# Attention and two feed-forward layers on one core: the halves of each split put in successive half blocks

## The chip, the cores and the metric

The kernel runs on one core of a Trainium2 chip. The metric is the device time of one execution in microseconds (us), the median over repeated runs. The core's engines are TensorE (PE), VectorE (DVE), ScalarE (ACT), GpSimd (POOL) and SyncE (SP); POOL and SP issue this kernel's DMAs.

## The reference

Each of 8 batches and 8 heads pools 576 keys and values with 32 packed queries, and attends from 576 queries to the 32 pooled rows. The result, 4608 tokens of 512 features, runs through a gated layer (1536 wide) and a cosine layer (2048 wide). All is float32.

```python
p_packed = sm_attn(p, k, v)            # softmax(p k^T / 8) v
out = sm_attn(q, p_packed, p_packed)
x = out, laid out as (4608, 512)
g = x @ w_gate
x = (silu(g) * (x @ w_val)) @ w_out
h = x @ w_in
return (h * cos(h)) @ w_out2
```

## The kernel before

A float32 value is kept as two fast-format parts: `hi` is a rounded copy that ACT writes (L86), and `lo` is the value minus `hi`, which DVE writes (L87). `split` issues both, one behind the other. A product then takes three passes over the parts, except in batch 0, which multiplies plain float32. Weights arrive packed; ACT unpacks a tile in two instructions (`decode_a`, L93 and L94) and DVE finishes it in two (`decode_b`, L100 and L103).

The program has three stages. The first is a loop over the batches b = 0 to 7 (`a_up`). Each batch has 12 blocks f, and each block two half blocks: the products `pg` (gate) and `pv` (value), 12 matmuls each (L456; L445 in batch 0). ACT takes silu of `pg` (L469), DVE multiplies it with `pv` into `h` (L482), and POOL stores `h`. The weights of a batch are not the plain gate and value weights but these multiplied by the batch's pooled rows: a projection `wp` (L425) makes them for two blocks at once, and is split. In batch 0 the projection is made block by block (`a_wp0`, L410, copied at L417).

Between the half blocks, `side(k)` with k = 0 to 23 issues what a table of numbers gives for place k. That is the attention of batch b + 1, whose steps are: scores and their maximum (`s1_mm`, `s1_max`), the exponential (`s1_exp`, on ACT), transposes (`a_t`, L185), the pooling product (`a_pp`, L195, with its scaling `ppu` on DVE, L202), its transpose, the second scores with their softmax (`s2_*`) and a split. It is also the projections, the loads, and the preparation of the later weights, one `w2_step` at a time: a list of 130 items, each a decoding, a split with a store (`w2_put`), or sums of tiles on DVE (L365). 98 items run in the first stage: 15 in each of batches 1 to 6 and 8 in batch 7. The last 32 run in the second stage.

The second stage is a product by Strassen's scheme (L562): five sets of tokens (512 wide but the fourth, which is 256), seven products each. While one product runs, ACT and DVE split the operands `g` of the next. The third stage is the second layer; the change leaves it alone.

On each engine instructions run in the order in which the program issues them. Products of the first two stages write to four PSUM buffers of two banks each; a product may start when the reader of the buffer's former contents is done. A tile may be read or rewritten only when the instruction of the other engine that it depends on is done.

Of the kernel before, what the change touches and what calls it, by code (L numbers as in the profile page):

```python
# [10 lines left out]
F32 = mybir.dt.float32  # L11
F32R = mybir.dt.float32r
# [33 lines left out]
def attention_mlp_kernel(ctx: ExitStack, tc: tile.TileContext, qT, kT, vP, pP, wgv, w12, out):  # L46
# [38 lines left out]
    def split(src, hi, lo, eng=DVE):  # L85
        ACT.activation(out=hi, in_=src, func=AF.Copy)  # L86
        eng.tensor_tensor(out=lo, in0=src, in1=hi.bitcast(F32), op=ALU.subtract)  # L87

    def like(x, out):
# [99 lines left out]
    def a_pp(b):  # L189
        pp = bank2("pp")  # L190
        for r in range(2):
            et = ET.pop(r)
            for c in range(NC):
                for i in range(4):
                    PE.matmul(  # L195
                        out=pp[cols(i), r, :64],
                        lhsT=et[:, c, cols(i)],
                        rhs=vt[b, 2 * r + i // 2][:, c, rows(i % 2)],
                        start=(c == 0), stop=(c == NC - 1),
                    )  # L200
            ppu[r] = st.tile([128, 2, 64], F32, tag="ppu", name="ppu", bufs=2)
# [4 lines left out]
        for j in range(NPAIR):  # L206
            del vt[b, j]

# [115 lines left out]
    NITEM = NW1 + 2 * NF2  # L324
    w2_end = [NW1 + NF2]
    w2_bufs = {"r": (ups, 3), "s": (ups, 7), "p": (ups, 3)}
# [12 lines left out]

    def w2_put(w_, dst):  # L340
        n = w_.shape[1]
        p = w2_new([128, n, 2, 256], F32R, "p", "w2p")
        split(w_, p[:, :, 0, :], p[:, :, 1, :])
        nc.gpsimd.dma_start(out=dst.rearrange("n p c -> p n c"), in_=p.bitcast(F32).rearrange("p n x c -> p n (x c)"))  # L344

    def w2_put_d(w_, dst):
        p = w2_new([128, 2, 512], F32R, "p", "w2p")
        split(w_.rearrange("p n c -> p (n c)"), p[:, 0, :], p[:, 1, :])
        nc.gpsimd.dma_start(out=dst, in_=p.bitcast(F32))

    def w2_decode(i):
        def go():
            w2_load(i + 2)
            w_, t_ = w2_tile("w2f"), w2_tile("w2t")
            raw = w2_raw.pop(i)
            decode_a(raw, t_.rearrange("p n c -> p (n c)"), w_.rearrange("p n c -> p (n c)"))
            decode_b(raw, t_.rearrange("p n c -> p (n c)"), w_.rearrange("p n c -> p (n c)"))
            w2_f[i] = w_
        return go

    def w2_pair(into, i):
        sub_, add_ = ALU.subtract, ALU.add

        def tt(o_, x, y, op):
            DVE.tensor_tensor(out=o_, in0=x, in1=y, op=op)  # L365

        def left():
            w2_put(w2_f[i], into[0:2])
# [7 lines left out]
        def put_a():  # L376
            w2_put(w2_f["a"], into[3:5])

        def sums_b():
            a, s_ = w2_f[i], w2_f["a"]  # L380
            r = w2_f["b"] = w2_tile("w2c")
            tt(r[:, 0], s_[:, 1], a[:, 0], sub_)
            tt(r[:, 1], a[:, 1], r[:, 0], sub_)
            w2_put(w2_f[i + 1][:, 1:2], into[2:3])

        def put_b():
            w2_put(w2_f["b"], into[5:7])
            for key in (i, i + 1, "a", "b"):
                del w2_f[key]

        return [w2_decode(i), left, w2_decode(i + 1), sums_a, put_a, sums_b, put_b]
# [5 lines left out]
    for n in range(NF2):  # L397
        w2_todo += [w2_decode(NW1 + NF2 + n), lambda n=n: w2_put_d(w2_f.pop(NW1 + NF2 + n), w2d[n])]

    def w2_step():  # L400
        if w2_todo:
            w2_todo.pop(0)()

# [14 lines left out]

    def a_wp(b, m):
        if b >= B:  # L420
            return
        p_ = bank2("wp")
        for c in range(4):
            for r in range(2):
                PE.matmul(  # L425
                    out=p_[cols(c), r, :],
                    lhsT=pp_of(b, r, c),
                    rhs=wg[m, c // 2][rows(r), c % 2].rearrange("p a n -> p (a n)"),
                    start=True, stop=True,
                )  # L430
        w_ = wp[b, m] = ups.tile([128, 2, 2, 512], F32R, tag="w", name="wp", bufs=4)
        split(p_, w_[:, :, 0, :], w_[:, :, 1, :])

    def a_up(b, sched):
        def side(k):
            for s_ in sched.get(k, ()):
                s_()

        def half(f, o, name):
            p_ = bank2(name)  # L440
            if b == 0:
                w = wp[0, f]
                for c in range(2):
                    for u in range(2):
                        PE.matmul(  # L445
# [3 lines left out]
                        )  # L449
                return p_[:, :, :HS]  # L450
            w, o = wp[b, f // 2], o + 256 * (f % 2)
            for c in range(2):
                n = 0
                for u in range(2):
                    for x, y in PASSES:
# [5 lines left out]
                        n += 1  # L461
            return p_[:, :, :HS]

        for f in range(NF1):
            pg = half(f, 0, "pg")
# [3 lines left out]
            ACT.activation(out=s_, in_=pg, func=AF.Silu)  # L469
# [7 lines left out]
            side(2 * f)  # L477
            pv = half(f, 128, "pv")
# [3 lines left out]
            DVE.tensor_tensor(out=h_, in0=s_, in1=pv, op=ALU.mult)  # L482
            nc.gpsimd.dma_start(out=h1[f, :, S * b:S * b + S], in_=h_.rearrange("p c n -> p (c n)"))  # L483
# [168 lines left out]
    with tc.manual_schedule():  # L652
# [25 lines left out]
        u_step(1, 1)  # L678
        a_pp(0)
        a_ppt(0)  # L680
        u_step(2, 1)
# [34 lines left out]
        def attention(sched, b, at_k):  # L716
            steps = (
                (lambda: s1_mm(b), lambda: s1_max(0), lambda: s1_max(1)), (s1_exp,), (s1_sum,), (a_t,),
                (lambda: a_pp(b),), (lambda: a_ppt(b),),
                (lambda: s2_mm(b), lambda: s2_turn(0), lambda: s2_turn(1)),  # L720
                (s2_max,), (s2_sub,), (s2_exp,), (s2_sum,), (s2_mul,), (lambda: s2_back(b),),
                (lambda: s2_split(b),), (lambda: a_wp(b, 0),), (lambda: a_wp(b, 1),),
            )
# [4 lines left out]
        for b in range(B):  # L728
            sched = {}
            if b == 0:  # L730
                for k, what in ((0, "k"), (2, "v"), (6, "q")):
                    put(sched, k, loads(1, what))
                attention(sched, 1, (3, 3, 6, 6, 8, 10, 12, 13, 14, 14, 16, 17, 18, 19, 20, 22))
                for k, what in ((12, "k"), (16, "v"), (20, "q")):
                    put(sched, k, loads(2, what))
                put(sched, 23, lambda: w2_load(0), lambda: w2_load(1))
            else:
                for m, k in ((2, 2), (3, 5), (4, 9), (5, 14)):
                    put(sched, k, lambda m=m: a_wp(b, m))
                if b < B - 1:  # L740
                    attention(sched, b + 1, (0, 1, 4, 4, 7, 8, 11, 12, 13, 13, 15, 16, 17, 18, 18, 21))
                    for k, what in ((6, "k"), (12, "v"), (16, "q")):
                        put(sched, k, loads(b + 2, what))
                    for k in (1, 2, 3, 4, 5, 6, 7, 8, 9, 10, 19, 20, 21, 22, 23):
                        put(sched, k, w2_step)
                else:
                    stage["att"].close()
                    late["da"] = pool("da")
                    for k in range(8):
                        put(sched, k, w2_step)  # L750
                    put(sched, 0, lambda: load_w1(0), lambda: g_first.append(new_g(512)), lambda: load_h(0, 0, 0))
# [16 lines left out]
        w2_end[0] = NITEM  # L768
        w2_load(NW1 + NF2)
        w2_load(NW1 + NF2 + 1)  # L770
        x_now = [None] * 7
# [4 lines left out]
        for s_ in range(len(SETS)):  # L776
            end = s_ == len(SETS) - 1
            for i in range(7):
# [249 lines left out]
```

## Time and profile before

| what | value |
|---|---|
| time, median of 3 runs (lowest to highest) | 1524.75 us (1523.59 to 1526.01) |
| the profiled execution: its time, its span | 1522.2 us, 1520.4 us |
| PE busy over the span | 1465.4 us (96%) |
| DVE busy | 1087.6 us (72%) |
| ACT busy | 850.2 us (56%) |
| DMA queue of SP, share of 16 engines | 51.8% |

Shares are averages over three stages with different limits. Ends of matmuls are modelled, so starts are the better measure on PE. A wait is put down to the releaser that came last.

### The profile page before, as it was taken

How to read it: one execution, taken by the hardware profiler on the slowest of the kernel's cores; microseconds unless marked ns; L12 is line 12 of the kernel's file. 1: busy time of each engine (PE TensorE's matmuls, PEld its weight loads, DVE VectorE, ACT ScalarE, POOL GpSimd, SP SyncE). 2: the span in 40 equal slices, each digit the busy share in tenths (PEclk: the TensorE clock that was granted, in tenths of full speed). 3: DMA queues.
4: the chain of work that ended last, by engine and by line, in shares of the span. 5: the costliest groups of instructions: out<-in, count | busy, mean ns of one | idle time of the engine just before them, and what ended most of it. 6: DMA issues, size and time to landing. Idle time of an engine off the chain costs nothing.

```text
span 1520.4 us, 25197 instructions
## 1 busy us (share of the span) xinstructions
PE 1465.4 (96%) x9432; PEld 1262.3 (83%) x9432; DVE 1087.6 (72%) x1767; ACT 850.2 (56%) x1501; POOL 123.9 (8%) x230
## 2 busy tenths in 40 slices
PE   8999899899899999999999999999999999999998
PEld 6667777777789788887888999999989998998997
DVE  6767776776775888988886775776776586677654
ACT  5765654565654455555475555555555464565642
POOL 0011221212221011011000000000000000000000
PEclk9999999999999999999999999999999999999999
DMA  8946855846588576466296586576667558656641
GB/s 317 341 169 231 292 210 196 307 178 226 208 300 326 219 253 246 156 215 242 92 381 215 172 257 225 176 226 198 201 208 254 167 175 284 199 174 193 203 157 42
DMA packets 140937, 335.64 MB, mean 221 GB/s; under 512 B 15248, under 2 KB 25488, under 8 KB 140816
## 3 DMA queue, kind: packets, MB, share of 16 engines
q1 hardware_dynamic: 120720, 262.19, 51.8%
q0 software_dynamic: 20096, 71.84, 12.2%
q8 instruction: 75, 1.23, 0.3%
q14 instruction: 46, 0.38, 0.1%
HBM read 252.71 MB, written 81.26 MB: 220 GB/s over the span
## 4 chain that ended last, share of the span: by engine, by line
PE 65%; issue 7%; DVE 5%; DMA 3%; ACT 3%; POOL 1%; SPq 0%; POOLq 0%; DVEq 0%; ACTq 0%
PE acc L891 26%; PE p L876 22%; PE o L562 14%; PE pg L456 2%; PE pv L456 1%; DMA hr<-h 1%; POOL h L483 1%; DMA w<-w1u 1%; DVE h L482 1%; POOL w2u L344 1%; DMA w2u<-w2p 1%; DVE wp L87 0%; DVE w2f L100 0%; PE wp L425 0%; DVE p L575 0%
## 5 line engine op out<-in xcount | busy, mean ns | idle before, releaser
L891 PE MATMUL acc<-wd,g 128*128 128x512 f32 x1728 | 418.1, 391 | 0.0
L876 PE MATMUL p<-xs,up 128*128 128x384 f32 x2016 | 379.5, 339 | 2.4 <-ACT p L951 1.9
L891 PEld LDWEIGHTS acc<-wd,g 128*128 128x128 f32 x1728 | 323.0, 188 | 61.4
L876 PEld LDWEIGHTS p<-xs,up 128*128 128x128 f32 x2016 | 358.9, 188 | 14.7 <-ACT p L951 2.8
L562 PE MATMUL o<-g,w 128*128 128x512 f32 (+1 forms) x1260 | 266.5, 373 | 7.2 <-DVE g L87 3.9
L562 PEld LDWEIGHTS o<-g,w 128*128 128x128 f32 x1260 | 220.6, 189 | 52.9 <-DVE g L87 5.5
L854 ACT ACTIVATE t<-c,quarter 128x384 f32<-128x384 f32 x144 | 88.6, 615 | 198.3 <-DVE c L964 192.6
L456 PEld LDWEIGHTS pv<-a,wp 128*128 128x128 f32 x1008 | 138.7, 189 | 26.3 <-DVE h L482 7.6
L86 ACT ACTIVATE g<-hr 128x1024 fp32r<-128x1024 f32 (+1 forms) x105 | 102.0, 976 | 101.4 <-PE o L562 54.1
L456 PE MATMUL pv<-a,wp 128*128 128x288 f32 x1008 | 152.7, 301 | 5.5 <-DVE h L482 4.9
L456 PEld LDWEIGHTS pg<-a,wp 128*128 128x128 f32 x1008 | 138.8, 189 | 21.1 <-issue 8.3
L456 PE MATMUL pg<-a,wp 128*128 128x288 f32 x1008 | 152.5, 300 | 0.3 <-DVE h L482 0.3
L87 DVE TENSOR_TENSOR g<-hr,g 128x1024 fp32r<-128x1024 f32 (+1 forms) x105 | 113.6, 1112 | 32.7 <-ACT g L86 32.5
L959 DVE TENSOR_TENSOR u<-v,p 128x384 f32<-128x384 f32 x48 | 26.6, 553 | 120.1 <-PE p L876 119.7
L864 DVE TENSOR_TENSOR g<-t,g 128x384 fp32r<-128x384 f32 x192 | 105.7, 550 | 8.6 <-ACT g L851 8.5
L469 ACT ACTIVATE silu<-pg 128x576 f32<-128x576 f32 x96 | 62.3, 649 | 82.8 <-PE pg L456 70.5
L856 DVE TENSOR_TENSOR t<-t,k 128x384 f32<-128x384 f32 x192 | 105.8, 551 | 3.5 <-ACT k L860 1.8
L857 ACT ACTIVATE t<-t 128x384 f32<-128x384 f32 x192 | 98.1, 511 | 2.5 <-DVE t L856 2.4
L851 ACT ACTIVATE g<-t 128x384 fp32r<-128x384 f32 x192 | 98.7, 514 | 0.4 <-DVE t L862 0.4
L905 DVE TENSOR_TENSOR oacc<-oacc,acc 128x512 f32<-128x512 f32 x108 | 73.7, 683 | 34.6 <-PE acc L891 34.6
L860 ACT ACTIVATE k<-t 128x384 int32<-128x384 f32 x192 | 98.1, 511 | 0.0
L87 DVE TENSOR_TENSOR wp<-wp 128x1024 fp32r<-128x1024 f32 x42 | 51.3, 1221 | 51.8 <-ACT wp L86 51.7
(101 smaller groups left out, 1488.4 us busy)
## 6 DMA issues: line engine op xcount, KB each, us to landing
up<-w2u SPq DMA_DIRECT2D x336, 256.0 KB, 3.1
wd<-w2d SPq DMA_DIRECT2D x96, 512.0 KB, 6.3
h<-h POOLq DMA_DIRECT2D x96, 288.0 KB, 4.7
hr<-h SPq DMA_DIRECT2D x48, 512.0 KB, 7.2
raw<-in_w SPq DMA_DIRECT2D x44, 512.0 KB, 4.8
raw<-in_wgv SPq DMA_DIRECT2D x24, 512.0 KB, 7.9
w2u<-w2p POOLq DMA_DIRECT2D x24, 512.0 KB, 5.1
w<-w1u SPq DMA_DIRECT2D x21, 512.0 KB, 11.2
```

The costliest lines, as they stand in the source:

```text
L86: ACT.activation(out=hi, in_=src, func=AF.Copy)
L87: eng.tensor_tensor(out=lo, in0=src, in1=hi.bitcast(F32), op=ALU.subtract)
L456: PE.matmul(out=p_[:, c, :HS], lhsT=w[:, u, x, o:o + 128], rhs=a2[b][:, u, y, HS * c:HS * c + HS], start=(n == 0), stop=(n == 5),)
L562: PE.matmul(out=acc[:, m, :N], lhsT=wd1[n, fp][:, j, 256 * x + 128 * m:256 * x + 128 * m + 128], rhs=g1[n, fp][:, y, j, :], start=(first a ...
L851: ACT.activation(out=three["g"][:, 0, :], in_=three["t"], func=AF.Copy)
L854: ACT.activation(out=now["t"], in_=now["h"], func=AF.Identity, scale=1.0 / TWO_PI, bias=quarter)
L856: DVE.tensor_tensor(out=one_["t"], in0=one_["t"], in1=one_["k"], op=ALU.subtract)
L857: ACT.activation(out=one_["t"], in_=one_["t"], func=AF.Sin, scale=SIN_SCALE)
L860: ACT.activation(out=now["k"], in_=now["t"], func=AF.Copy)
L864: DVE.tensor_tensor(out=three["g"][:, 1, :], in0=three["t"], in1=three["g"][:, 0, :].bitcast(F32), op=ALU.subtract)
L876: PE.matmul(out=out, lhsT=w[:, u, 128 * k:128 * k + 128], rhs=x[:, v, k, :], start=(first and k == 0 and i == 0), stop=(last and k == 1 an ...
L891: PE.matmul(out=acc, lhsT=gs[p, a, t][:, x, o:o + 128], rhs=wd[j, f][:, y, :], start=(f == 0 and n == 0), stop=(f == 3 and n == 2),)
```

## The change

Each split and each decoding of the first stage, and the preparation of the later weights in both stages, is issued in two parts. ACT's instruction is issued at its place k; DVE's instruction and the store behind it are issued at the next place (`pend`) or at the next `w2_step` (`w2_flush`). The scaling of the pooling product becomes a step of its own, behind all 80 matmuls of that product. Attention has 20 steps in place of 16, at other places. In batch 0 projections are made for two blocks at once from block 2 on, and the first block's four products with the first half of the features come ahead of those with the second half. Of the list of 130 items, 110 now run in the first stage (17 in each of batches 1 to 6, 8 in batch 7); the 20 that are left run in the first three sets of the second stage, one to a product, and none in the last two sets.

```diff
+    def split_later(src, hi, lo, then=None):
+        ACT.activation(out=hi, in_=src, func=AF.Copy)
+
+        def go():
+            DVE.tensor_tensor(out=lo, in0=src, in1=hi.bitcast(F32), op=ALU.subtract)
+            if then:
+                then()
+        return go
...
     def a_pp(b):
-        pp = bank2("pp")
+        pp = s1_["pp"] = bank2("pp")
...
+    def a_ppu():
+        pp = s1_.pop("pp")
+        for r in range(2):
             ppu[r] = st.tile([128, 2, 64], F32, tag="ppu", name="ppu", bufs=2)
...
     def s2_split(b):
...
-            split(s2_["af"], a2[b][:, :, 0, :], a2[b][:, :, 1, :])
+            pend.append(split_later(s2_["af"], a2[b][:, :, 0, :], a2[b][:, :, 1, :]))
...
-    w2_end = [NW1 + NF2]
+    w2_end = [NW1 + NF2 + 6]
...
             decode_a(raw, t_, w_)
-            decode_b(raw, t_, w_)
-            w2_f[i] = w_
+            return lambda: decode_b(raw, t_, w_)
...
     def w2_step():
+        w2_flush()
         if w2_todo:
-            w2_todo.pop(0)()
+            w2_dve.append(w2_todo.pop(0)())
...
     def a_wp(b, m):
...
-        split(p_, w_[:, :, 0, :], w_[:, :, 1, :])
+        pend.append(split_later(p_, w_[:, :, 0, :], w_[:, :, 1, :]))
 
     def a_up(b, sched):
         def side(k):
+            now = pend[:]
+            del pend[:]
+            for s_ in now:
+                s_()
             for s_ in sched.get(k, ()):
                 s_()
...
-                if f + 1 < NF1:
-                    a_wp0(f + 1)
+                if f == 0:
+                    a_wp0(1)
+                elif f % 2:
+                    if f + 1 < NF1:
+                        a_wp0_pair((f + 1) // 2)
...
-                    attention(sched, b + 1, (0, 1, 4, 4, 7, 8, 11, 12, 13, 13, 15, 16, 17, 18, 18, 21))
+                    attention(sched, b + 1, (0, 1, 2, 5, 6, 8, 9, 10, 12, 13, 14, 15, 16, 18, 19, 20, 21, 17, 19, 22))
...
-                    for k in (1, 2, 3, 4, 5, 6, 7, 8, 9, 10, 19, 20, 21, 22, 23):
+                for k in (0, 3, 4, 5, 5, 6, 7, 7, 8, 9, 10, 11, 11, 12, 17, 21, 23) if b < B - 1 else range(8):
...
-                if s_ or i > 2:
-                    for _ in range(2 if i in (1, 6) else 1):
-                        w2_step()
+                if s_ < 3 or i < 3:
+                    w2_step()
```

The order of instructions shows the move at three places, all in batch 3. First DVE around the first projection of the batch; the names are those of the words above, `mx` and `nm` the maxima of the scores, `w2f` a decoded tile. Before, from `h` of block 0:

```order
L482 TENSOR_TENSOR h<-silu,pv 128x576
L100 SCALAR_TENSOR_TENSOR w2f<-w2t,w2f 128x512
L103 SCALAR_TENSOR_TENSOR w2f<-raw,w2f 128x512
L87 TENSOR_TENSOR wp<-wp 128x2x512
L365 TENSOR_TENSOR w2c<-w2f 128x256 x2
L482 TENSOR_TENSOR h<-silu,pv 128x576
L87 TENSOR_TENSOR w2p<-w2c,w2p 128x2x256
```

Now, from `h` of block 1:

```order
L550 TENSOR_TENSOR h<-silu,pv 128x576
L99 TENSOR_TENSOR w2p<-w2c,w2p 128x2x256
L115 SCALAR_TENSOR_TENSOR w2f<-w2t,w2f 128x512
L118 SCALAR_TENSOR_TENSOR w2f<-raw,w2f 128x512
L550 TENSOR_TENSOR h<-silu,pv 128x576
L99 TENSOR_TENSOR wp<-wp 128x2x512
L115 SCALAR_TENSOR_TENSOR w2f<-w2t,w2f 128x512
L118 SCALAR_TENSOR_TENSOR w2f<-raw,w2f 128x512
L99 TENSOR_TENSOR w2p<-w2f,w2p 128x2x256
```

The row `wp<-wp`, which needs ACT's copy of the same projection, stood behind a decoding that needs ACT too, and ahead of `h` of block 1. Now it stands behind `h` of block 2, one half block after the copy, and two decodings stand around it.

Second, ACT at the same place. Before, from silu of block 0 to that of block 2:

```order
L469 ACTIVATE silu<-pg 128x576
L169 ACT_TABLE_LOAD
L169 ACTIVATE E,sm<-s_2429,nm 128x576
L169 ACTIVATE E,sm<-s_2430,nm 128x576
L93 ACTIVATE w2t<-raw 128x512
L94 ACTIVATE w2f<-raw,low_87 128x512
L469 ACT_TABLE_LOAD
L469 ACTIVATE silu<-pg 128x576
L86 ACTIVATE wp<-wp 128x2x512
L86 ACTIVATE w2p<-w2c 128x2x256
L469 ACTIVATE silu<-pg 128x576
```

Now, from silu of block 1 to the copies in block 2:

```order
L530 ACTIVATE silu<-pg 128x576
L184 ACT_TABLE_LOAD
L184 ACTIVATE E,sm<-s_2406,nm 128x576
L184 ACTIVATE E,sm<-s_2407,nm 128x576
L108 ACTIVATE w2t<-raw 128x512
L109 ACTIVATE w2f<-raw,low_87 128x512
L530 ACT_TABLE_LOAD
L530 ACTIVATE silu<-pg 128x576
L108 ACTIVATE w2t<-raw 128x512
L109 ACTIVATE w2f<-raw,low_87 128x512
L96 ACTIVATE wp<-wp 128x2x512
L96 ACTIVATE w2p<-w2f 128x2x256
L96 ACTIVATE w2p<-w2f 128x256
```

The exponential with its two table loads comes one half block later, a second decoding stands ahead of the projection's copy, and two copies for stores follow it.

Third, PE at the pooling product, with what each row waits for (`DVE_49` and `Activation_49` are signals of DVE and ACT, `PE_49` of PE itself, `DMAHW` of loads). Before:

```order
L195 MATMUL pp<-vt,ET 32x64 [waits DMAHW3_49,DVE_49]
L195 MATMUL pp<-vt,ET 32x64
L195 MATMUL pp<-vt,ET 32x64 [waits DMAHW4_49]
L195 MATMUL pp<-vt,ET 32x64 x17
L195 MATMUL pp<-vt,ET 32x64 [waits DMAHW5_49,DVE_49]
L195 MATMUL pp<-vt,ET 32x64
L195 MATMUL pp<-vt,ET 32x64 [waits DMAHW6_49]
L195 MATMUL pp<-vt,ET 32x64 x17
L456 MATMUL pg<-a_2282,wp 128x288 [waits Activation_49]
```

Now:

```order
L210 MATMUL pp<-vt,ET 32x64 [waits DMAHW5_49,Activation_49]
L210 MATMUL pp<-vt,ET 32x64
L210 MATMUL pp<-vt,ET 32x64 [waits DMAHW6_49]
L210 MATMUL pp<-vt,ET 32x64 x17
L210 MATMUL pp<-vt,ET 32x64 [waits DMAHW7_49,Activation_49]
L210 MATMUL pp<-vt,ET 32x64
L210 MATMUL pp<-vt,ET 32x64 [waits DMAHW0_49]
L210 MATMUL pp<-vt,ET 32x64 x17
L510 MATMUL pv<-a_2336,wp 128x288 [waits PE_49]
```

The second half of the product waited for DVE, which had to read the first half out of the same buffer; now it waits for ACT's copy of the transposes.

## Rows read from the trace of the kernel before

**Rows 1.** Busy time by window: us, PE, PEld, DVE, ACT, POOL, granted clock, DMA
```profile
26.00:96.80 70.80, 64.79 (x557) 41.93 (x557) 53.13 (x82) 52.99 (x82) 6.33 (x13) 0.98 0.82 287
96.80:442.00 345.20, 313.93 (x3242) 261.95 (x3241) 246.72 (x378) 198.11 (x287) 73.96 (x133) 0.99 0.64 228
485.80:660.00 174.20, 172.79 (x747) 140.12 (x747) 148.84 (x154) 95.55 (x120) 17.90 (x33) 1.00 0.63 226
660.00:712.00 52.00, 46.19 (x311) 42.03 (x310) 43.90 (x66) 30.18 (x52) 8.68 (x16) 0.97 0.75 271
```

**Rows 2.** Waits of PE, 96.8 to 442 us: total, times, longest
```profile
PE pp L195 <- DVE ppu L202: 10.4, 6, 2.1
PE wp L425 <- ACT silu L469: 7.0, 5, 1.8
PE tp L185 <- DVE wp L87: 5.6, 6, 1.4
```

**Rows 3.** Waits of DVE for ACT, same stretch and columns
```profile
DVE wp L87 <- ACT wp L86: 48.2, 21, 4.1
DVE w2p L87 <- ACT w2p L86: 15.5, 17, 2.3
DVE w2f L100 <- ACT w2f L94: 15.0, 9, 3.0
DVE a L87 <- ACT a L86: 7.4, 6, 1.2
```

**Rows 4.** Timeline of PE, batch 3: start, us, instructions, idle before
```profile
222.59 0.77 PE L185 MATMUL tp<-ident,E 128*128 128x128 f32 x5 [1.41 <-DVE wp L87]
223.92 3.25 PE L456 MATMUL pv<-a,wp 128*128 128x288 f32 x12 [0.56 <-DVE h L482]
227.10 1.09 PE L425 MATMUL wp<-wg,ppT 64*32 64x512 f32 x16
251.92 1.76 PE L456 MATMUL pg<-a,wp 128*128 128x288 f32 x12
253.52 1.76 PE L456 MATMUL pv<-a,wp 128*128 128x288 f32 x12
```

**Rows 5.** Timeline of ACT, batch 4, and two rows of DVE
```profile
266.79 1.01 ACT L86 ACTIVATE wp<-wp 128x1024 fp32r<-128x1024 f32 x1
267.69 0.66 ACT L93 ACTIVATE w2t<-raw 128x512 f32<-128x512 f32 x1
268.91 0.64 ACT L469 ACTIVATE silu<-pg 128x576 f32<-128x576 f32 x1
275.04 1.28 ACT L169 ACT_TABLE_LOAD   x1 [1.91 <-DVE nm L161]
276.33 0.74 ACT L169 ACTIVATE E<-s,nm 128x576 f32<-128x576 f32 x1
277.90 1.28 ACT L469 ACT_TABLE_LOAD   x1
...
269.32 0.68 DVE L100 SCALAR_TENSOR_TENSOR w2f<-w2t,w2f 128x512 uint32<-128x512 uint32 x1
280.80 1.23 DVE L87 TENSOR_TENSOR wp<-wp 128x1024 fp32r<-128x1024 f32 x1 [3.61 <-ACT wp L86]
```

**Rows 6.** Waits of PE, 485.8 to 712 us, and one row of its timeline
```profile
PE o L562 <- DVE g L87: 3.9, 5, 1.4
PE o L562 <- ACT g L86: 3.3, 2, 2.2
...
706.64 0.49 PE L562 MATMUL o<-g,w 128*128 128x512 f32 x1 [2.16 <-ACT g L86]
```

**Rows 7.** Timeline of PE in batch 0
```profile
28.68 2.80 PE L445 MATMUL pg<-af,wpf 128*128 128x288 f32 x6 [1.93 <-DVE af L277]
62.14 0.66 PE L410 MATMUL wp<-wg,ppT 64*32 64x256 f32 x16
93.99 1.09 PE L425 MATMUL wp<-wg,ppT 64*32 64x512 f32 x16
```

More of the change, by code (lines that the diff above doesn't have):

```diff
@@ L200, in a_pp @@
                     )
+        for j in range(NPAIR):
+            del vt[b, j]
+    def a_ppu():
+        pp = s1_.pop("pp")
+        for r in range(2):
             ppu[r] = st.tile([128, 2, 64], F32, tag="ppu", name="ppu", bufs=2)
@@ L383, in sums_b, with right_and_sums @@
             tt(r[:, 1], a[:, 1], r[:, 0], sub_)
[L384 to L391, printed above, removed]
+            del w2_f[i], w2_f[i + 1]
+        right = w2_put(lambda: w2_f[i + 1][:, 1:2], into[2:3])
+        def right_and_sums():
+            lo = right()
+            return lambda: (lo(), sums_a())
+        return [
+            w2_decode(i), w2_decode(i + 1), w2_put(lambda: w2_f[i], into[0:2]), right_and_sums, lambda: sums_b,
+            w2_put(lambda: w2_f.pop("a"), into[3:5]), w2_put(lambda: w2_f.pop("b"), into[5:7]),
+        ]
     for n in range(NP1):
@@ L396, in attention_mlp_kernel, with w2_flush @@
         w2_todo += w2_pair(w2u[n], NW1 + 2 * n)
-    for n in range(NF2):
-        w2_todo += [w2_decode(NW1 + NF2 + n), lambda n=n: w2_put_d(w2_f.pop(NW1 + NF2 + n), w2d[n])]
+    for n in range(0, NF2, 2):
+        i = NW1 + NF2 + n
+        w2_todo += [w2_decode(i), w2_decode(i + 1), w2_put_d(i, w2d[n]), w2_put_d(i + 1, w2d[n + 1])]
+    w2_dve = []
+    def w2_flush():
+        while w2_dve:
+            w2_dve.pop(0)()
     def w2_step():
+        w2_flush()
         if w2_todo:
-            w2_todo.pop(0)()
+            w2_dve.append(w2_todo.pop(0)())
     wp = {}
@@ L417, in a_wp0, with a_wp0_pair, wp_mm @@
         ACT.activation(out=wp[0, f], in_=p_[:, :, :256], func=AF.Copy)
-    def a_wp(b, m):
-        if b >= B:
-            return
+    wp0 = []
+    def a_wp0_pair(m):
+        if not wp0:
+            wp0.append(ups.tile([128, 2, 2, 512], F32, tag="a2", name="wpp", bufs=2))
+        p_ = wp_mm(0, m)
+        w_ = wp0[0][:, m % 2]
+        ACT.activation(out=w_, in_=p_, func=AF.Copy)
+        for f in (2 * m, 2 * m + 1):
+            wp[0, f] = w_[:, :, 256 * (f % 2):256 * (f % 2) + 256]
+    def wp_mm(b, m):
         p_ = bank2("wp")
@@ L430, in a_wp, with half @@
                 )
+        return p_
+    def a_wp(b, m):
+        if b >= B:
+            return
+        p_ = wp_mm(b, m)
         w_ = wp[b, m] = ups.tile([128, 2, 2, 512], F32R, tag="w", name="wp", bufs=4)
-        split(p_, w_[:, :, 0, :], w_[:, :, 1, :])
+        pend.append(split_later(p_, w_[:, :, 0, :], w_[:, :, 1, :]))
     def a_up(b, sched):
         def side(k):
+            now = pend[:]
+            del pend[:]
+            for s_ in now:
+                s_()
             for s_ in sched.get(k, ()):
                 s_()
-        def half(f, o, name):
-            p_ = bank2(name)
+        def half(f, o, p_, us=(0, 1)):
             if b == 0:
                 w = wp[0, f]
-                for c in range(2):
-                    for u in range(2):
+                for u in us:
+                    for c in range(2):
                         PE.matmul(
@@ L461, in half @@
                         n += 1
-            return p_[:, :, :HS]
         for f in range(NF1):
-            pg = half(f, 0, "pg")
+            first = b == 0 and f == 0
+            pg = bank2("pg")
+            if first:
+                pv = bank2("pv")
+                half(f, 0, pg, (0,))
+                half(f, 128, pv, (0,))
+                half(f, 0, pg, (1,))
+            else:
+                half(f, 0, pg)
             if b == 0 and f:
@@ L477, in a_up @@
             side(2 * f)
-            pv = half(f, 128, "pv")
+            if first:
+                half(f, 128, pv, (1,))
+            else:
+                pv = bank2("pv")
+                half(f, 128, pv)
             if b == 0 and f:
```

81 lines of the change are left out of this document (45 added, 36 removed).

## The prediction

> **What bounds the kernel now.** I read the windows by stage first, then the waits of PE, then those of DVE in the stretch that the change rewrites, and last the timelines there.
>
> The windows [rows 1] show where PE stands still. Batches 1 to 6 take 345.2 us, in which PE is busy for 313.9: 31.3 idle, the largest lump in the run. Batch 0 has 6.0 (70.8 less 64.8), the first three sets of the second stage 1.4, and the window round its narrow fourth set 5.8. The third stage is not touched. The granted clock is 0.99 and 0.97 where PE waits most.
>
> The waits of PE [rows 2] name the 31.3: the pooling product's second half for DVE's `ppu` (10.4, six times), projections for ACT's silu (7.0), transposes for DVE's `lo` of a projection (5.6), and smaller ones of the same kind. So DVE and ACT free the PSUM buffers late. Why, when DVE is busy for only 246.7 of 345.2 us? Its waits for ACT [rows 3] answer: 48.2 + 15.5 + 15.0 + 7.4 = 86.1 us it stands in front of the `lo` half of a split or the second half of a decoding. 246.7 + 86.1 is 332.8 of 345.2. DVE has no slack in this stage: it works through its queue in order, and the hand-over from ACT inside the queue is its loss. That is the loss the change goes for.
>
> A second price hangs on the waits. After the gaps of 1.41 and 0.56 us in batch 3, a `pv` half block takes 3.18 us from start to start (223.92 to 227.10) where an undisturbed one takes 1.60 [rows 4]. That is the lower of the two clock levels, 1.2 in place of 2.4 GHz. 1.6 us is one such loss; the mean clock of 0.99 over 345.2 us allows up to 3.5. I take 3.0 for batches 1 to 6, and for the fourth set 0.03 x 52.0, 1.6 us, by its row in [rows 1].
>
> **Batches 1 to 6.** At stake: 31.3 + 3.0 = 34.3 us. Removed for certain is the wait inside the pooling product: all 80 matmuls are issued before DVE reads the buffer, so the 10.4 go [rows 2]. What is added is two list items per batch: a decoding (two of 0.68, 1.3 with their overlap) and a split of half the width of the 1.23 in [rows 5] are 2 us of DVE, far less than the 86.1 / 6 = 14.4 us per batch that it stood waiting. DVE's work still fits under PE's 52 us a batch (313.9 / 6).
>
> What is late next? I walked batch 3 through the three queues with durations of the timelines; two places stay. The first is the exponential. Let T = 0 be the end of block 1's `pg`. ACT then does silu (0.64), a table load (1.28), two exponentials (276.33 to 277.90, 1.57), a decoding (267.69 to 268.91, 1.22), the load back (1.28), silu of block 2, a second decoding (1.22), and only then the copy of the projection (1.01) [rows 5]: 0.64 + 1.28 + 1.57 + 1.22 + 1.28 + 0.64 + 1.22 + 1.01 = 8.9. DVE's `lo` adds 1.23 [rows 5] and frees the buffer at 10.1. PE meanwhile does `pv`, `pg`, the projection, `pv`, `pg` (four half blocks at 1.60, 1.09 for the projection) and ten transposes (1.4, by 0.77 for five less overlap) [rows 4]: 8.9. The next `pv` needs that buffer and waits 1.2; with the time that signals take on ACT's and DVE's side I count 1.4.
>
> The second is a hand-over the other way. Behind the projection's copy ACT has two copies for stores, and the second needs a tile that DVE decodes behind that same `lo`: DVE is ready at 10.1 + 1.3 = 11.4 [rows 5]. ACT, whose first copy is half as wide as the 1.01, has been free since 9.4. It stands for 2.0, then does the second copy (a quarter, 0.3) and silu of block 3, done at 12.4. `pg` of block 4, due at 10.1 + 1.6 = 11.7, waits 0.7. Elsewhere the walk finds 0.3, in all 2.4 us in this batch. Its position in the list is the heaviest one: two decodings in this spot; the other batches have one or none there. I take 2.0 a batch, 12.0 in all. No row shows the new order, so the bounds are 0 (all buffers in time) and 5.0 a batch, 30 in all (nearly today's 31.3 / 6 = 5.2). **Gain 34.3 - 12.0 = 22.3.**
>
> Here a page of the Trainium skill speaks against the change. The row first: after the load at 275.04, lasting 1.28, the exponential starts at 276.33 [rows 5], so a switch of tables costs 1.3 us. "ScalarE: Activation LUTs", section "What ACT_TABLE_LOAD costs", counts a drain of about 1.38 us on top of a load of 1.283 for every switch. By that estimate the first place, with two switches ahead of the copy, would wait 2.8 longer in each batch, and six batches would give back 16.6 of the gain. The trace does not show the drain, and the sum goes by the row.
>
> **Batches 0 and 7.** Eleven single projections of 0.66 become one single and five double ones of 1.09 [rows 7]: 7.3 less 6.1 is 1.2, or less with overlap; I take 0.9. One projection moves from batch 7 to batch 0, at no net cost. The first block's wait of 1.93 for the features [rows 7] gets three more products ahead of it, half a us each (eight matmul rows in some 2 us): 1.5 gained. Against it the double projection needs block 3's weights decoded two blocks early, which I reckon at 2.0 of new wait, between nothing and the four instructions of a decoding twice over, 5. Of the idle time of batch 0 that is not the 1.93 (4.1) I take 1.5 as gone, since the pooling product no longer waits inside and ACT copies less; batch 7 gives 0.3. **Gain** 0.9 + 1.5 - 2.0 + 1.5 + 0.3 = **2.2**, between -2 and 6.
>
> **The second stage.** PE waits 7.2 there for the operands `g`, 3.9 for DVE and 3.3 for ACT [rows 6]; 5.8 of it lies round the fourth set [rows 1], whose products are half as long while the list costs DVE the same. Nine of the 32 items ran there before, none does now. The load of the next set's tokens, issued when DVE frees their tile, moves ahead with them, and the wait at 706.64 (2.16) is for it [rows 6]. I take 5.0 of 5.8, and 1.0 of the 1.6 of clock. The first products now carry items that they didn't: one a product is hidden, since DVE is busy for 148.8 of 174.2 us there and the items fell from 23 to 20 in these three sets. If that cover is gone, a decoding's 1.3 us shows at up to three products. **Gain 6.0**, between 2 and 8.
>
> **The sum.** 22.3 + 2.2 + 6.0 = 30.5. The profiled execution took 1522.2 us (span 1520.4), so 1491.7; the median of the runs shown is 2.55 above it, so I forecast 1494.
>
> **The rivals.** *ACT becomes the late engine.* It has lost nothing of its four table loads per batch, and the places found above are both its own. If every batch loses 4.5 and not 2.0, 15 us of gain go: 1509. For it speaks the walk, against it that ACT is busy for only 198.1 of 345.2. The page above would do just this, by its own figures: 1511.
>
> *The waits only move.* DVE's halves are later than before by half a block, so buffers are held longer, and PE loses elsewhere what it got from the pooling product. The second stage's 6.0 stay: 1518. Against it: 86 us of standing cannot stay if ACT's halves are ahead.
>
> *No waits at all.* Zero for the 12.0 left in batches 1 to 6, and batch 0 at its best: 1478.
>
> *Slower: the hand-over turns round.* ACT's copies for stores wait for DVE's decodings and sums, and silu stands behind them. The price is 2.0 each, as at the second place. The table doubles items at k = 5, 7 and 11, where ACT meets DVE's half at once. With four such stalls a batch not hidden and the 1.4 of the first place: 9.4 a batch, 56 in all, less 34.3 + 2.2 + 6.0: 1539. It decides from 7.1 us of waits a batch (42.5 / 6). In the walk only one of these stalls reached PE, and with 0.7.
>
> **Chances.** Forecast 0.58, ACT late 0.17, waits move 0.07, no waits 0.10, slower 0.06, no measurable change 0.02. A measurement of this kernel can tell about 0.2%, 3 us. Faster 0.92, same 0.02, slower 0.06. The range is 1480 to 1512: it takes the forecast with its bounds, nearly all of the late ACT, and half of the case without waits.
>
> **What would show it.** Right: the pooling product in one run of 80 matmuls with no wait; DVE's waits for ACT in batches 1 to 6 down from 86 us to under 25; PE's waits there at 8 to 16 us, the largest `pv` of block 3 behind a projection's `lo`, and `pg` of block 4 behind silu; a batch at 53 to 54 us and not 57.5; the fourth set without its 5.8. Wrong: ACT standing for DVE by more than 5 us a batch, `pg` waiting for silu in most blocks, or new waits of the first set's products for `g`.

## The result, and the profile after

The changed kernel takes 1539.39 us (median of three, 1536.52 to 1540.94) against 1524.75: ratio 1.0093, 95% interval 1.0066 to 1.012. It is 0.9% slower; 1494 was forecast. The profiled execution has a span of 1537.6 us, 17.2 more than before, and a mean granted clock of 0.989 in place of 0.996.

Busy time by window of the changed kernel, cut at the first product of batch 0, of batch 1, of batch 7, of the second stage and of the third (columns as in [rows 1]):

```profile
26.20:101.00 74.80, 68.59 (x494) 41.07 (x492) 53.36 (x82) 53.36 (x78) 6.34 (x13) 1.00 0.77 271
101.00:438.80 337.80, 313.66 (x3242) 262.15 (x3241) 256.65 (x400) 206.57 (x303) 79.27 (x140) 0.99 0.67 240
438.80:489.90 51.10, 44.07 (x337) 39.93 (x337) 25.88 (x34) 21.55 (x32) 9.79 (x18) 0.93 0.98 364
489.90:772.40 282.50, 267.98 (x1262) 221.47 (x1261) 219.79 (x239) 137.10 (x178) 26.61 (x49) 0.98 0.51 180
772.40:1537.60 765.20, 755.25 (x3745) 681.75 (x3743) 518.76 (x986) 420.21 (x890) 1.08 (x2) 1.00 0.63 204
```

The last three of these stretches in the kernel before:

```profile
442.10:485.80 43.70, 43.44 (x355) 39.14 (x354) 25.63 (x38) 20.04 (x30) 11.69 (x20) 1.00 0.87 335
485.80:759.40 273.60, 266.38 (x1262) 220.62 (x1262) 230.58 (x257) 147.84 (x196) 29.84 (x55) 0.99 0.59 209
759.40:1520.40 761.00, 754.12 (x3745) 680.09 (x3743) 518.58 (x986) 420.15 (x890) 1.08 (x2) 1.00 0.63 206
```

So the loss has an address, and it is not where the change was aimed at. Two columns of runs that come later are set beside it ("all mends" is the run in which four mends, one for each loss, are put together):

| stretch, us | before | changed | four store buffers | all mends |
|---|---|---|---|---|
| batch 0 | 70.8 | 74.8 | 74.9 | 68.6 |
| batches 1 to 6 | 345.3 | 337.8 | 317.1 | 320.9 |
| batch 7 | 43.7 | 51.1 | 51.4 | 42.9 |
| second stage | 273.6 | 282.5 | 282.5 | 264.4 |
| third stage | 761.0 | 765.2 | 764.8 | 761.0 |

Batches 1 to 6 gain 7.5 us; the four others lose 4.0 + 7.4 + 8.9 + 4.2 = 24.5, and 0.2 lies ahead of batch 0.

**Batches 1 to 6.** The waits from 101 to 438.8 us of PE, ACT and DVE (total, times, longest):

```profile
PE pg L510 <- ACT silu L530: 8.8, 9, 1.9
PE ppt L231 <- DVE ppu L223: 7.4, 3, 4.9
...
ACT w2p L96 <- DMA w1u<-w2p: 19.2, 5, 5.9
ACT w2p L96 <- DMA w2u<-w2p: 15.9, 5, 6.7
ACT a L96 <- DVE af L294: 12.8, 6, 2.8
...
DVE w2p L99 <- ACT w2p L96: 19.9, 10, 5.7
DVE wp L99 <- ACT wp L96: 17.2, 14, 2.7
DVE w2f L115 <- ACT w2f L109: 7.5, 9, 1.8
```

DVE's waits in front of these second halves fell from 86.1 us [rows 3] to 44.6, so the hand-over is better, if not by as much as hoped; in front of `h` its waits for ACT rose from 2.4 to 13.7. New is that ACT stands 35.1 us in front of a `w2p` split for the store of what that buffer held before; it was 2.8. There are three such buffers, which the splits take in turn, as a ring. The timeline of batch 5 shows one of these ten waits, first ACT, then DVE, then PE:

```profile
342.21 0.63 ACT L96 ACTIVATE w2p<-w2f 128x512 fp32r<-128x512 f32 x1 [1.41 <-DVE w2f L118]
...
343.59 0.42 ACT L96 ACTIVATE w2p<-w2f 128x256 fp32r<-128x256 f32 x1 [0.20 <-ACT silu L530]
...
346.38 0.63 ACT L96 ACTIVATE w2p<-w2c 128x512 fp32r<-128x512 f32 x1 [1.18 <-issue]
...
354.23 0.63 ACT L96 ACTIVATE w2p<-w2c 128x512 fp32r<-128x512 f32 x1 [6.68 <-DMA w2u<-w2p]
...
354.89 0.69 DVE L99 TENSOR_TENSOR w2p<-w2c,w2p 128x512 fp32r<-128x512 f32 x1 [5.71 <-ACT w2p L96]
355.50 0.61 DVE L223 TENSOR_SCALAR ppu<-pp,rs 128x128 f32<-128x128 f32 x2
...
356.00 0.66 PE L231 MATMUL ppt<-ident,ppu 128*128 128x128 f32 x2 [4.87 <-DVE ppu L223]
356.31 3.23 PE L510 MATMUL pv<-a,wp 128*128 128x288 f32 x12
359.34 2.87 PE L510 MATMUL pg<-a,wp 128*128 128x288 f32 x12
```

ACT's fourth split in a row needs the first one's buffer. ACT stands 6.68, DVE stands 5.71 for ACT, the pooling product's scaling stands behind that on DVE, and PE waits 4.87 for it. The next `pv` then takes 3.03 from start to start where 1.60 is usual: the lower of the two clock levels, 1.2 GHz (the granted clock is 0.58 from 356 to 363 us).

**Batch 7.** SP's queue and its wait (total, times, longest, from 418 to 450 us), then ACT and PE, then the landing times of the packed-weight loads from 430 to 600 us:

```profile
395.94 43.33 SPq L354 DMA_DIRECT2D raw<-in_w  x5
439.44 1.41 SPq L568 DMA_DIRECT2D w<-w1u  x3
...
SPq L354 <- DVE w2f L118: 32.2, 3, 18.8
...
461.48 0.66 ACT L108 ACTIVATE w2t<-raw 128x512 f32<-128x512 f32 x1 [7.50 <-DMA raw<-in_w]
...
463.37 1.96 PE L470 MATMUL wp<-wg,ppT 64*32 64x512 f32 x16 [5.89 <-ACT silu L530]
...
DMA to landing us min/median/max: 3.5/4.6/15.6
```

A load of packed weights (`raw`) may go out when DVE's half of an older decoding has read the buffer, and that half is now issued up to five places later. SP stands for it (18.8 us the longest time), and with it all that is queued behind. In the kernel before, the first weights of the second stage left SP 23.5 us ahead of batch 7, now 0.6 after its start:

```profile
418.56 1.42 SPq L500 DMA_DIRECT2D w<-w1u  x3
```

The next `raw` load is then issued behind six transfers of 0.5 MB, lands 15.6 us later, and ACT, with silu behind it, stands 7.5.

**The second stage.** ACT, PE and SP in the first two sets:

```profile
511.37 0.66 ACT L108 ACTIVATE w2t<-raw 128x512 f32<-128x512 f32 x1 [14.70 <-DMA raw<-in_w]
...
514.63 0.80 PE L630 MATMUL o<-g,w 128*128 128x512 f32 x1 [6.97 <-ACT g L86]
572.22 0.80 PE L630 MATMUL o<-g,w 128*128 128x512 f32 x1 [5.19 <-ACT g L86]
...
551.80 0.35 SPq L354 DMA_DIRECT2D raw<-in_w  x1
552.20 3.12 SPq L581 DMA_DIRECT2D hr<-h  x6
```

The first set's decoding now comes with its first product, and its `raw` load is queued behind nine loads of 0.5 MB. ACT stands 14.70, and the copies for the next product stand behind it. The second wait is SP's again: token loads (`hr`) queue behind a `raw` load that waits for DVE's late half. In the narrow set nothing is left of the 5.8 us [rows 1, 6]: from 582 to 772 us PE waits 0.8.

**The third stage**, which the diff does not touch, has one new wait. PE, then DVE and ACT:

```profile
772.43 1.21 PE L943 MATMUL p<-xs,up 128*128 128x384 f32 x6
777.73 2.79 PE L943 MATMUL p<-xs,up 128*128 128x384 f32 x9 [4.09 <-ACT p L1018]
...
776.36 1.28 DVE L643 TENSOR_TENSOR p<-p,o 128x512 f32<-128x512 f32 x2
...
776.53 0.49 ACT L1018 ACTIVATE p<-p 128x384 f32<-128x384 f32 x1 [2.22 <-DVE xs L87]
```

The profile names ACT, whose copy was done at 777.02. What ends at 777.64 is DVE's sum over the last product of the second stage. In the built program that product lies in PSUM banks 6 and 7, and the second product of the third stage takes bank 7. Before the change it lay in banks 2 and 3.

**Batch 0.** The fourth of its five double projections, broken, and an unbroken one of batch 1:

```profile
73.18 1.06 PE L470 MATMUL wp<-wg,ppT 64*32 64x512 f32 x8
74.58 1.06 PE L470 MATMUL wp<-wg,ppT 64*32 64x512 f32 x8 [0.34 <-DVE wg L118]
...
82.95 1.09 PE L470 MATMUL wp<-wg,ppT 64*32 64x512 f32 x16
```

A pair that must wait for the second half of its weights takes 2.39 from start to the next instruction (75.57), an unbroken one 1.02. PE's waits for `wg` are 3.9 us in all, 3.1 of them at the pairs, and four of the five pairs are broken.

### The profile page after: what moved, and what is told of

It is laid out like the page before. It is cut to its first block, busy times and chain, and to the rows that moved or that the text cites. A ratio compares the mean times of both kernels' runs of the same rounds, so it can differ in the third digit from the quotient of the medians.

```text
span 1537.6 us, 25005 instructions
## 1 busy us (share of the span) xinstructions
PE 1472.7 (96%) x9352; PEld 1265.6 (82%) x9352; DVE 1087.3 (71%) x1767; ACT 849.9 (55%) x1496; POOL 124.0 (8%) x230
## 4 chain that ended last, share of the span: by engine, by line
PE 63%; DMA 2%; DVE 2%; ACT 1%; issue 1%; SPq 0%; ACTq 0%; DVEq 0%
PE acc L958 26%; PE p L943 22%; PE o L630 14%; DMA hr<-h 2%; DMA raw<-in_w 1%; PE pg L510 1%; PE pv L510 1%; DVE g L87 0%; ACT g L86 0%; DVE xs L87 0%; DVE p L643 0%; ACT k L927 0%; DVE xt L690 0%; ACT t L921 0%; PE wp L470 0%
## 5 line engine op out<-in xcount | busy, mean ns | idle before, releaser
L550 DVE TENSOR_TENSOR h<-silu,pv 128x576 f32<-128x576 f32 x96 | 71.5, 745 | 47.7 <-PE pv L510 14.2
```

## The experiments

Theory after the comparison: four separate losses (store buffers, SP's queue in batch 7 and in the second stage, broken pairs, PSUM banks). Main rival: that of the prediction, ACT standing for DVE, which had given 1539 too. "Of before" means the kernel before on the same chip.

**A buffer against the turned ring (first try).**

```diff
+        bank2("skip")
         for n in ("db", "da", "ps"):
```

> One PSUM buffer is taken and left unused just before the third stage, so that its first products fall on the banks on which they fell before the change. Theory (the changed number of projections in batch 0, seven in place of twelve, turned the ring of four buffers, and a first product of the third stage lands on the bank that the last product of the second stage still holds): the wait of 4.09 us at 773.6 and the slow clock behind it go, the time falls by 4 to 5 us against the changed kernel, to 1534.5 to 1535.5, and nothing ahead of the third stage moves. Rival (the wait is for weights that land late, or a chance of that one execution): no change, 1539.

1540.22 us, span 1537.6. The buffer was never written, so it was dropped from the program. The run is a repeat of the changed kernel (1.0108 of before, 1.0086 to 1.013) and tells nothing of the theory.

**Packed weights first, second stage.**

```diff
+        w2_load(NW1 + NF2 + 6)
+        w2_load(NW1 + NF2 + 7)
         load_h(0, 1, 1)
...
-        w2_load(NW1 + NF2 + 6)
-        w2_load(NW1 + NF2 + 7)
```

> At the start of the second stage the two loads of packed weights go to SP's queue ahead of the two token loads and the nine weight loads of the first set, and not behind them. Theory (ACT stands 14.7 us for a packed weight in the first set, with the copies for the next product behind it): that wait falls below 3 us, PE's wait of 6.97 at 507.7 and the slow clock behind it go, 7 to 9 us off the changed kernel's time, 1530 to 1532; the wait of 5.19 at 567 stays. Rival (the transfers share one saturated stretch, so that the first set waits for its own weights or tokens instead): under 2 us off. Rival of the prediction (ACT's waits for DVE in batches 1 to 6 make the loss): no change here, 1539.

1536.18 us, 1.0086 (1.0058 to 1.0114): about 4 off, half of what was expected. ACT's wait is gone; PE waits 4.05 us for DVE instead, which stood 5.26 us for tokens, whose loads were now behind. The rival has half of it: the DMA engines are full in this stretch (share 1.06 in the changed kernel from 499 to 508 us), and this order made others wait. That no order could do better is not shown, and the run on the second stage below says the opposite.

**Later loads in batch 7.**

```diff
-                    put(sched, 0, lambda: load_w1(0), ...
+                    put(sched, 3, lambda: load_w1(0), ...
-                    put(sched, 4, lambda: load_w1(4))
+                    put(sched, 6, lambda: load_w1(4))
```

> In batch 7 the loads of the first two products' weights and of the first tokens are issued at places 3 and 6 in place of 0 and 4, behind the two loads of packed weights. Theory (the second of these lands 15.6 us after its issue because six transfers of 0.5 MB lie ahead of it; ACT stands 7.5 us for it and PE 5.9): both waits go, batch 7 takes 44 to 45 us in place of 51.1, and 6 to 7 us come off, 1532 to 1533. Rival (the DMA engines are full throughout batch 7, so the wait goes to the start of the second stage): batch 7 is shorter, but the first set waits as much longer, 1537 to 1540.

1.0108 of before (1.0073 to 1.0142; three executions, 1535.89 to 1544.11 us): no gain, as the rival had it. Where the wait went is not shown. The other direction, earlier loads, was tried below.

**Four store buffers.**

```diff
-    w2_bufs = {"r": (ups, 3), "s": (ups, 7), "p": (ups, 3)}
+    w2_bufs = {"r": (ups, 3), "s": (ups, 6), "p": (ups, 4)}
```

> Four buffers in place of three for the split weights that wait to be stored, one less for decoded ones. Theory (ACT stands 35.1 us in batches 1 to 6 in front of splits whose buffer is still being stored, because a store now goes out one step later and the splits follow each other closer; silu and the pooling product's scaling stand behind it): these waits fall under 10 us, PE's waits of 24 us there by a third to a half, and 8 to 12 us come off with the clock, 1527 to 1531. Rival (PE's waits there come from the order of the steps, the exponential and the hand-over from DVE to ACT): ACT's waits for stores go but turn into waits for DVE and PE, under 3 us off.

1519.51 us, 0.9975 (0.9963 to 0.9987): 20 us off the changed kernel, more than expected. ACT's waits in batches 1 to 6:

```profile
ACT w2p L96 <- DMA w2u<-w2p: 2.7, 2, 1.7
ACT w2p L96 <- DMA w1u<-w2p: 1.1, 1, 1.1
```

35.1 has become 3.8, PE's waits went from 24.2 to 7.5, DVE's for ACT from 44.6 to 22.6, and the six batches from 337.8 to 317.1; what is more than the waits is the clock, as PE's busy time fell from 313.7 to 309.5. In front of `h` DVE still waits 14.3 for ACT. All other stretches stay as they were. One buffer decided the sign.

**The PSUM ring, turned by a product of zeros** (on top of four store buffers, as the next three).

```diff
+                    put(sched, 20, lambda: keep_busy(1))
```

> With four store buffers as in the run before, and one product of zeros (128 columns) into a PSUM buffer of its own at place 20 of batch 7. It turns the ring, so that the last product of the second stage lies in banks 2 and 3, as in the kernel before the change, and not in 6 and 7, of which the third stage's second product takes 7. (The earlier try left its buffer unused, and an unused buffer is dropped when the program is put together: it was the changed kernel once more.) Theory: the 4.09 us in front of the second product and the slow clock behind it go, the third stage takes 761 us in place of 764.8, the run is 3.5 to 4.5 us shorter than with four store buffers alone (0.9975 of the kernel before): 1515 to 1516, 0.995. Rival (weights land late there): no change.

1516.34 us, 0.9963 (0.995 to 0.9976), and the start of the third stage in PE's timeline:

```profile
755.75 4.40 PE L944 MATMUL p<-xs,up 128*128 128x384 f32 x24
```

24 matmuls without a wait, and 1516.8 - 755.75 = 761.05 us for the stage: the theory, to the size. In the built program the last product lies in banks 2 and 3.

**SP's queue ahead of batch 7.**

```diff
+            w2_flush()
             now = pend[:]
...
+                    put(sched, 0, lambda: load_w1(0), ..., lambda: load_h(0, 0, 0))
                 for k in ... range(8):
                     put(sched, k, w2_step)
...
-                    put(sched, 0, lambda: load_w1(0), ..., lambda: load_h(0, 0, 0))
```

> With four store buffers. DVE's half of a decoding or split of the later weights is issued at the next place, not at the next such step (up to five places later), and in batch 7 the loads of the first product's weights and tokens go to SP's queue ahead of the load of a packed weight. Theory (SP stood 10.5 us in front of that load, which waits for DVE's late half, and the loads of the second stage began at the start of batch 7 and not 7 us earlier): the loads begin 5 to 7 us ahead of batch 7, ACT's wait for a packed weight falls from 10.4 to under 4 us, batch 7 takes 44 to 47 us in place of 51.4: 1513 to 1515, 0.991 to 0.993. Rival (the DMA engines are full from there to the first set, whatever the order): batch 7 shorter, the first set longer, under 2 us off.

1510.03 us, 0.9921 (0.9906 to 0.9935). SP's first weights, and ACT's wait in batch 7, which starts at 420.2:

```profile
402.18 1.55 SPq L569 DMA_DIRECT2D w<-w1u  x3
...
433.13 0.68 ACT L108 ACTIVATE w2t<-raw 128x512 f32<-128x512 f32 x1 [0.88 <-DMA raw<-in_w]
```

Batch 7 takes 42.9 us, less than before the change. The weights leave SP 18 us ahead of it, and ACT waits 0.9: the theory, with more than it asked for. The second stage takes 283.8, 1.3 more than with four buffers alone, so the rival has at most that. The six batches take 317.9, 0.8 more than with four buffers alone, and batch 0 76.6, 1.7 more, and no run shows why. The gain is not all batch 7's 8.5: the third stage is 3.6 shorter, since the last product of the second stage now lies in banks 4 and 5, and PE waits 1.94 there in place of 4.09. (The run with later loads had pushed in the wrong direction.)

**The second stage.**

```diff
-            w2_load(i + 2)
+            if not w2_late:
+                w2_load(i + 2)
...
+                if w2_late:
+                    w2_load(i + 2)
...
+        w2_late.append(1)
...
-                if s_ < 3 or i < 3:
-                    w2_step()
+                if s_ < 3 and (s_ or i > 2):
+                    for _ in range(2 if i in (1, 6) else 1):
+                        w2_step()
```

> With four store buffers. In the second stage a packed weight is loaded with DVE's half of a decoding and not with ACT's, so that SP need not stand for the half that comes one product later; and the first set starts its items with its fourth product, two at two products of a set, as in the kernel before. Theory (ACT's wait of 14.7 for a packed weight and the token loads queued behind packed ones on SP make PE's two waits of 5 to 7 us with the slow clock behind each): the second stage takes 266 to 270 us in place of 282.5, under the 273.6 of the kernel before, since the narrow set still has no items: 1504 to 1508, 0.988. Rival (the first set is short of its own transfers): only the second wait goes, 1512.

1501.76 us, 0.9874 (0.9855 to 0.9893). The stage takes 263.5 us, and PE's only wait of it is:

```profile
PE o L637 <- DVE g L87: 0.5, 1, 0.5
```

Both long waits are gone, and the granted clock over the stage is 1.00 in place of 0.98: the stage is 2.5 us better than the best that was expected. Which of the two edits removed which wait was not parted.

**Single projections in batch 0.**

```diff
-                if f == 0:
-                    a_wp0(1)
-                elif f % 2:
-                    if f + 1 < NF1:
-                        a_wp0_pair((f + 1) // 2)
+                if f + 1 < NF1:
+                    a_wp0(f + 1)
```

> With four store buffers. Batch 0 makes its projections block by block again, the rest as changed. Theory (the pair needs weights decoded one block earlier; PE waits 3.9 us for them, and a pair that is broken by the wait takes 2.1 us and not 1.09, four times): batch 0 takes 70 to 71.5 us in place of 74.9. The ring turns too: the last product of the second stage now lies in banks 0 and 1, and the third stage's first product takes 0, so it waits for the last sum itself and the third stage is 0 to 2 us longer than 764.8: 1515 to 1518 in all, 0.995. Rival (the waits of batch 0 come from the places of the attention steps): batch 0 stays at 74 to 75.

1515.85 us, 0.9955 (0.9939 to 0.9971). Batch 0 takes 68.6 us, less than the 70.8 of before: what else changed in batch 0 gains 2.2, and the pairs lose 6.3. (Batches 1 to 6 take 318.3, 1.2 more than with four buffers alone.) And the third stage begins as the bank theory says for banks 0 and 1, with its first product waiting, for which the profile names no releaser; DVE's sum over the last product ends at 752.69:

```profile
752.79 14.24 PE L940 MATMUL p<-xs,up 128*128 128x384 f32 x70 [5.15 <-issue]
...
751.41 1.28 DVE L640 TENSOR_TENSOR p<-p,o 128x512 f32<-128x512 f32 x2
```

**All mends together.** The edits of four store buffers, of SP's queue, of the second stage and of single projections (with single projections the last product lies in banks 2 and 3, so no product of zeros).

> All together: four store buffers, DVE's half of the later weights at the next place and the first loads of batch 7 ahead of the packed weights, packed weights of the second stage loaded with DVE's half and its items from the fourth product on, single projections in batch 0 (with which the ring of PSUM buffers ends as in the kernel before). Theory (four separate losses, which add): with four buffers alone the span was 1516.3; less 8.5 in batch 7, 19.0 in the second stage, 6.3 in batch 0 and 3.7 in the third stage, as the single runs showed them: 1479, and 1476 to 1486 with overlaps, 0.970 to 0.976 of the kernel before. Rival (batch 7 and the first set share one full stretch of transfers, so two of the gains are one): 1486 to 1494.

1485.41 us, 0.9746 (0.972 to 0.9773): faster than both kernels, by 37 and by 54 us. The span, 1483.6, is 4.8 over the sum, mostly the 3.8 by which batches 1 to 6 are longer than with four buffers alone (320.9). The gains add but for these 4.8. The time lies at the lower edge of the rival's range, but the stages decide against it: batch 7 and the second stage take 42.9 and 264.4, where the single runs had 42.9 and 263.5. Whether the mends other than the fourth buffer would also help the kernel before was not tried.

**Halves together, else as changed** (three store buffers).

```diff
             w2_dve.append(w2_todo.pop(0)())
+            w2_flush()
...
-            now = pend[:]
-            del pend[:]
-            for s_ in now:
-                s_()
             for s_ in sched.get(k, ()):
                 s_()
+                while pend:
+                    pend.pop(0)()
```

> The changed kernel (three store buffers) with DVE's half, and the store behind it, issued at once behind ACT's half, as in the kernel before; steps, items and places stay as changed. If the deferral alone overfills the ring of store buffers: ACT's waits for stores in batches 1 to 6 fall from 35.1 us to under 10, while DVE's waits for ACT go back above 60 us from 44.6 (w2p, wp, w2f). If the new order of the items does it (splits closer to each other): ACT still waits over 20 us for stores. In both cases the ring of PSUM buffers ends on banks 0 and 1, so the third stage pays 5 us, and the second stage's late loads go, as SP no longer waits for the late half: 1525 to 1540 in all.

1531.41 us, 1.0052 (1.0037 to 1.0066). ACT's waits for stores in batches 1 to 6:

```profile
ACT w2p L96 <- DMA w1u<-w2p: 14.0, 3, 5.2
ACT w2p L96 <- DMA w2u<-w2p: 7.7, 3, 4.6
```

21.7 of the 35.1 stay, so it is mostly the new order of the items that overfills the ring, and the deferral adds 13.4. The changed list puts the two decodings of a pair of weights first and its four splits behind them, with one step of sums between; before, a decoding and a step of sums stood between the first split and the others. The table also doubles places; the two were not parted. DVE's waits for ACT are 67.9 us, as expected above 60. The six batches take 347.3, 9.5 more than as changed, but batch 7 takes 42.9, since SP's first weights leave 8.3 us ahead of it and not behind its start. Of the 9.5 that the deferral gains in the six batches, batch 7 gives back 8.2 and the later stages 6.0, so this run is the shorter one of the two.

The third stage's first product waits 5.14, with the last product in banks 0 and 1, as expected. What was expected of the second stage holds in part: PE's second wait is gone, but ACT still stands 14.6 us for a packed weight in the first set, and PE 6.6 behind it. The first set's wait, then, comes from the item in its first product and the queue ahead of its load, not from late halves.

**Four store buffers in the kernel before.** The same line as above, in the old kernel.

> The kernel before with four store buffers and one buffer less for decoded weights. Theory (there ACT waited only 2.8 us for stores, so the ring bound nothing and became the bound through the change): no difference, 0.998 to 1.002 of the kernel before. Rival (a fourth buffer helps either kernel, so that the change gains nothing of its own): 0.990 or less.

0.9998 (0.9982 to 1.0014): no difference. The ring was no bound until the change made it one.

**All mends, halves together.**

> As the run with all mends, but DVE's halves issued at once behind ACT's. Theory of the prediction (DVE standing for ACT's half is what delays the buffers that PE needs): DVE's waits for ACT in batches 1 to 6 rise from some 24 us to over 60, PE's waits there from 7 or 8 us to 15 to 30, and the run is 10 to 25 us longer than that one. Rival (the spread of the attention steps and the pooling product's scaling as its own step do it, the halves' places matter little): under 5 us longer.

1493.08 us, 0.9801 (0.9773 to 0.9829): 7.7 longer than with deferred halves, between theory and rival. DVE's waits for ACT are 49.4 us in place of 20.9 (in front of `h` it waits 12.3 for ACT with deferred halves, and not at all here), PE's 16.3 in place of 8.7, the largest of them:

```profile
PE ppt L231 <- DVE ppu L223: 7.5, 6, 1.9
```

The six batches take 327.0 against 320.9. Of the 24.4 us that they gain over the kernel before, the deferred halves bring 6.1. The other 18.3 come with the halves together: from the spread of the steps, the undivided pooling product and the new places of the items, which no run parts.

## Why the prediction was wrong

**What bounds the kernel: right in the place, and in part in the cause.** With four store buffers batches 1 to 6 gain 345.3 - 317.1 = 28.2, where 22.3 was forecast, and DVE's waits in front of second halves are 22.6 (under 25 was the mark). But the prediction called DVE's standing for ACT the loss that the change goes for, and the last run gives the deferred halves only 6.1 of 24.4. That 28.2 is near the forecast is in part luck. The walk through batch 3 found the right two places, though over the six batches `pv` waited for a projection's `lo` only twice. PE in the changed kernel:

```profile
232.14 1.85 PE L510 MATMUL pv<-a,wp 128*128 128x288 f32 x12 [1.57 <-DVE wp L99]
234.51 1.73 PE L510 MATMUL pg<-a,wp 128*128 128x288 f32 x11 [0.51 <-ACT silu L530]
```

1.4 and 0.7 were forecast. By an estimate from the drain of about 1.38 us a switch that the Trainium skill states ("ScalarE: Activation LUTs", "What ACT_TABLE_LOAD costs") the first would be 2.8 longer. The trace does not agree: a load follows a copy and silu follows the load with no gap for a drain.

```profile
334.90 0.62 ACT L96 ACTIVATE w2p<-w2c 128x512 fp32r<-128x512 f32 x1
335.54 1.28 ACT L530 ACT_TABLE_LOAD   x1
336.83 0.65 ACT L530 ACTIVATE silu<-pg 128x576 f32<-128x576 f32 x1
```

**The failed step of this term: "two list items per batch ... are 2 us of DVE".** The kernel as changed gained 7.5 here, not 22.3. The step priced the items on DVE alone. Each split also holds a buffer until POOL's store of it has landed, and the new order takes four in a row from a ring of three. ACT stood 35.1 us for stores, and one more buffer takes 20.7 us off the six batches. The 2.8 us that ACT waited for a store before was the row to ask.

**Batches 0 and 7, forecast 2.2 gained, measured 11.4 lost.** "Decoded two blocks early, which I reckon at 2.0 of new wait", with bounds of nothing and 5, held for the wait (3.1 at the pairs) but not the price of the work: a pair was taken at 1.09 unbroken, and costs 2.1 without its wait when broken. "Batch 7 gives 0.3" left SP out: nobody asked what the later DVE half holds up on the queue of loads.

**The second stage, forecast 6.0 gained, measured 8.9 lost.** The narrow set gave its 5.8 as forecast. "One a product is hidden, since DVE is busy for 148.8 of 174.2" failed: the item was not late on DVE. Its load was late on SP, and ACT stood 14.70 us for the load.

**"The third stage is not touched": 4.2 lost**, by the order in which buffers were taken and released long before.

**The rivals.** "The hand-over turns round" gave 1539, the time measured, and is still wrong. ACT's waits for DVE in batches 1 to 6 fell from 61.0 us (`a` 21.5, `w2c` 12.7, `d` 11.0, `nm` 10.1, `w2f` 5.7) to 28.6 (`a` 12.8, `w2c` 9.6, `w2f` 6.2). That the time came out is luck: this rival put the whole loss into batches 1 to 6, which gained 7.5. Of the marks for "wrong", ACT stood 4.8 us a batch for DVE (over 5 was the mark), and `pg` waited for silu in 9 of 72 blocks, not in most; new waits of the first set for `g` did come, through SP's queue. "ACT late" was nearer, with another cause.

## What to carry to other kernels

When an instruction is issued later, list what its end releases, on every queue: the buffer, the store behind it, the load that refills the buffer, and all that stands behind that load. Count a ring's buffers against the longest run of takers in the new order and the landing time of a store (from issue to arrival), not against the average. And look at stages that the diff does not touch for what they inherit: the order of transfers and the banks that were last in use.

## What the runs showed that was not expected

- A projection of 16 matmuls in 64x32 tiles takes 1.02 us in one piece, and its halves 1.06 and 0.99 when a wait parts them (the fourth pair of batch 0): halves that run apart cost as much as the whole.
- PSUM buffers pass from one stage to the next in an order that depends on what was taken and released long before. The same wait cost 5.15 us with the last product in banks 0 and 1, 4.09 in 6 and 7, 1.94 in 4 and 5 (run on SP's queue) and none in 2 and 3.
- After gaps of 4 to 7 us PE came back at the lower clock level for a part of the time: in the changed kernel the mean granted clock was 0.80 from 514.6 to 525 us, 0.76 from 572 to 582, 0.60 from 777.7 to 782.
